# A Winograd residual block: first loads in one order with three in flight, half of image 2's squares on ScalarE, embedding weights in the staging buffers, and a new instruction order

## The chip, the cores and the metric

One Trainium2 chip, one core of it. The metric is the device time of one execution in microseconds. Before the change it is 475.57 us, the median of 3 runs (474.12 to 476.09).

## The reference

A residual block of a diffusion network on x of 2 images x 512 channels x 64 x 64, in bfloat16. `gn` is a group norm over 4 groups of 128 channels, `conv3` a 3x3 convolution from 512 to 512 channels with zero padding.

```python
h = conv3(silu(gn(x, g1, be1)), w1)
emb = silu(t_emb) @ w_emb              # t_emb: 2 x 1152, w_emb: 1152 x 512
h = h + emb.reshape(B, C, 1, 1)
h = conv3(silu(gn(h, g2, be2)), w2)
return x + h
```

A group of the norm is one channel tile of 128 channels, the partitions of the chip. So the mean and the mean square of a channel tile are sums along its 4096 pixels and over its partitions.

## The kernel before

**Tiling.** There are 4 channel tiles (ct) on the input side and 4 (ot) on the output side. An image is cut into 2 chunks of 32 rows, so each convolution ("layer") has 4 chunks, and each chunk 4 groups, one for each ot: 32 groups in all. The convolution is done by a Winograd scheme along the rows (4 output rows from 6 transformed rows, "pos" 0 to 5), and for some positions also along the columns ("nested"). The transformed activations of a chunk are V, made by VectorE and ScalarE; the transformed weights are U, made from the raw weights R and a third tap g1t. Positions 0 and 5 use R itself.

**The work of a chunk's V** (`produce_V`): for each channel tile, a load into `ak` (chunk 0 uses the x that is there already, `xbuf`), the SiLU with the norm's scale and bias on ScalarE (L571), a scaling by -4 (L578 and L584 through the helper at L300/L301), an addition (L585), a subtraction (L592), a doubling, then the rows of V (L612, L622) and its column differences (L632, L637). There are two V buffers: a chunk's V begins when the last matmul of the chunk two before has read its own. `xbuf` takes the first of them at the start.

**The work of a weight block's U** (`prep_U`, one for each pair of channel tiles): loads of g1t (L393) and R (L394), scalings (L300/L301), an addition that is a DMA of GpSimd (L424) or VectorE's, and two additions on VectorE (L413). g1t stays in one of 3 staging buffers ("stage") until its last addition.

**Scaled copies.** The string FLIP says for each scaled copy, in the order in which the program is written, whether ScalarE (L300) or VectorE (L301) does it.

**The norm's statistics.** For image 1 (`stats0`) and image 2 (`gn1_stats`) TensorE computes the Gram matrix of a channel tile's pixels in 32 matmuls of 128 columns (L354); VectorE takes its diagonal (L363), the sum of squares. 32 matmuls against a column of ones give the sums (L359). For channel tile 0 of image 1 ScalarE makes the sums (L703). `gn_scale_bias` turns both into scale and bias: a matmul over the partitions (L311), a few small steps of VectorE (L313 to L328) and a power on GpSimd (L326). Image 2's pixels come in 8 pieces of 512 KB into the 5 slots of `ring` (`gn1_load`, L477). They wait for the last load of image 1, and a slot's second piece for those who read the first.

**The output of a group.** ScalarE or VectorE moves the sums out of PSUM (`rm`), VectorE combines rows into `ring` slots 0 to 2 (y) and 3 and 4 (z), GpSimd adds z to y with a DMA (L983), and SP stores y to `h_scr` (L987). In layer 0 ScalarE then sums y and its squares (L748).

**The embedding.** w_emb comes in 5 loads (four of 256 KB, one of 128 KB, L451) into stretches of a V buffer that its chunk does not use, one before each of the groups 2 to 6. `emb_mm` multiplies them one group later (L460).

**The order.** Each engine executes its instructions in a fixed order. A table ORDER, one list of ranks for each of TensorE, VectorE, ScalarE, GpSimd and SP, was written down beforehand and is laid over the program by `in_order`. SP issues nearly all loads and stores, so a wait in front of one holds up all that stand behind it. There are 8 semaphores for SP's and ScalarE's DMAs, and a DMA that takes a semaphore again waits for the landing of the one before.

SP's first loads stand in this order: the two halves of image 1's channel tile 0 (512 KB each), tiles 1 and 2 (1 MB each), R of the first weight pair, tile 3, g1t of the first pair, R and g1t of the second.

Of the kernel before, what the change touches and what calls it, by code (L numbers as in the profile page):

```python
# [10 lines left out]
ALU = mybir.AluOpType  # L11
# [7 lines left out]
class _Background:  # L19
# [45 lines left out]
0-31 34 66 35-38 32 39-46 33 47-60 67-95 61-65 96-97 99-106 98 107-158 164-167 159-162 168-194 163 195 228 196-227  # L65
230-242 294 229 300-302 243 295-299 303-304 382 306-308 305 385 309 383 386 310 384 311 244-291 376 292-293 377 387
378 388 379-381 458-461 389 462-463 390 312-354 467 355-364 464 391-393 365-375 470-475 540 465 541 466 552-553 542
394-414 554 415 555 543-545 416-456 556-557 457 468-469 546-548 476-539 549-551 558 582 559 583 560 584 561-565
585-592 566-570 593 606-611 618-619 612-617 620 571-574 594 575-577 595-596 578-581 597-605 621 630 622-625 631
646-648 626 662-667 627-629 668-675 649-654 676-677 655-661 632-635 678-680 636-640 681-684 641-642 685 687-690  # L70
643-645 691 699-704 692 705 693-696 706 686 711-713 727 707-708 743 709-710 697 744 714 745 715-721 698 722-726
746-754 728-742 755-756 775-776 787 777 757-763 767 788-790 768 764-766 791-795 778 796-797 799 779 800 798 801-806
815 780-783 807 784 808-810 816-817 785 769 811-812 770 818 786 819-820 813-814 821-823 771-773 824 774 825-858
863-868 859 869-874 887 903 888 904-908 889-892 909-912 893 860-862 913 875-881 919 882 920 883 921 914-917 922-923
918 924-926 894 884-886 927-928 895-899 929 900-902 930-932 951-955 933-936 963 937-942 964-966 956 967 957 968 958
969 943-944 970 975-976 959 991 960 971 961-962 992 945 972 946-950 993-996 973 997-998 974 999 977 1000 1007-1017
1039 1051 1018-1021 1001 1022-1029 1002 1030 1003-1004 1040-1043 978 1005-1006 1044 979-981 1045 982 1052 1046 983
1053 984-990 1047 1054 1048-1049 1055-1056 1050 1057-1060 1031-1038 1061 1063-1067 1079 1068 1095 1062 1096-1111
1069 1112 1070-1078 1113-1118 1080-1094 1123 1135-1138 1119 1139 1120-1122 1140-1142 1124-1128 1147 1129 1148-1153
1163-1171 1154-1156 1172-1174 1157-1162 1130 1175 1143 1131 1176-1178 1144-1145 1132-1133 1146 1134 1179-1181  # L80
1195-1203 1182-1184 1204-1210 1185-1194 1211 1223-1225 1212-1218 1226-1231 1219-1222 1232-1239 1251 1240-1250
1252-1272 1283-1298 1273-1279 1299-1301 1311 1280-1282 1302-1305 1312-1313 1306-1307 1314-1316 1308 1317 1323 1339
1355 1340-1354 1318-1319 1309-1310 1320-1322 1324-1338 1356-1365 1387 1366-1368 1388 1369 1371-1381 1370 1382-1384
1399 1385-1386 1389 1400 1411-1413 1401 1414-1416 1402 1427 1443 1428-1430 1417 1431-1436 1418-1426 1437-1442 1444
1403 1445-1452 1404-1405 1390-1392 1406-1410 1393-1398 1459-1466 1475 1467-1474 1453-1458 1476-1477 1488-1496
1500-1501 1497-1498 1502 1499 1516-1524 1503-1515 1478-1487 1525-1526 1532 1527-1531 1533-1536 1564-1569 1576
1537-1541 1577-1580 1548-1563 1542-1547 1581 1570 1582 1571-1573 1583-1587 1574-1575 1588-1590 1604 1591-1594
1605-1608 1595-1603 1609-1635 1652-1655 1664 1656 1665 1657 1636-1651 1666-1669 1658-1660 1676-1677 1670 1678
1671-1672 1679 1673-1674 1680-1686 1692-1694 1687-1688 1695-1696 1708-1709 1689 1697-1704 1690 1710 1705-1706 1691
1707 1675 1661-1663 1711-1739 1764-1765 1740-1750 1766 1751-1757 1767-1768 1758-1759 1769 1760 1770 1761-1763  # L90
1771-1780 1796-1799 1781 1800-1801 1782 1802-1804 1783-1795 1828 1805-1806 1829 1812 1830-1831 1813 1807-1809 1832
1810 1814-1823 1811 1824-1827 1852 1833-1834 1840 1853-1854 1835-1836 1841-1842 1837-1838 1843-1845 1868 1846 1839
1869-1871 1847-1850 1872-1873 1855-1856 1851 1874-1877 1857-1862 1884 1863-1867 1885-1907 1878-1883 1932-1934
1908-1912 1935-1944 1920-1921 1945-1947 1922-1928 1913 1929-1931 1948-1953 1964-1966 1954-1957 1914-1919 1967
1958-1963 1968-1985 1988-1992 1986-1987 1993-1997 2000 1998 2001-2005 2012-2013 2028 2014-2016 2044-2046 2017
2029-2032 2006 2033-2035 2018-2022 1999 2036 2023-2024 2037-2038 2025 2039-2041 2047 2042 2007-2011 2026-2027
2048-2056 2068-2070 2080 2071-2073 2043 2074 2057 2075-2077 2081-2083 2078-2079 2058-2067 2084-2086 2092-2093
2108-2110 2087 2094 2088-2090 2124-2125 2091 2126-2131 2111-2114 2095-2098 2132 2099 2115 2133 2100-2102 2116-2120
2103 2121-2123 2134 2104 2149 2105-2107 2150-2153 2161-2162 2135 2163 2154 2164 2148 2165 2173-2174 2136-2140 2175
2141-2144 2166 2145-2147 2167-2168 2155-2156 2169-2170 2189 2171 2157-2160 2176 2190-2191 2177-2180 2192 2181-2186  # L100
2193 2187 2205 2194 2188 2195 2172 2206-2210 2196-2204 2211 2221-2236 2212-2220 2237-2240 2249-2250 2241-2242
2251-2252 2243-2244 2253-2254 2245 2255 2246-2248 2256-2261 2277 2262-2267 2293 2268-2270 2278-2281 2271-2275 2325
2276 2282-2292 2294-2305 2337 2306 2326 2338-2339 2307-2308 2340 2327-2331 2341 2309-2324 2349-2361 2365-2370
2362-2363 2371-2375 2342 2364 2376 2381-2382 2377-2380 2343 2332-2336 2344 2383-2385 2345-2348 2386-2412 2437
2413-2427 2438-2443 2428-2430 2453-2460 2469 2461-2468 2444-2452 2431-2436 2470-2478 2501-2503 2479-2484 2504-2508
2485-2500 2509-2510 2513-2515 2511 2525-2526 2516-2518 2512 2519-2520 2527 2521-2522 2541-2542 2557-2559 2528 2543
2529-2532 2523 2533 2560 2544 2561-2562 2545 2524 2546-2547 2534-2536 2548-2549 2537-2538 2550 2539 2551-2552 2540
2553-2556 2563-2572 2589-2595 2573-2576 2601-2605 2577-2588 2596-2598 2613-2615 2599-2600 2606-2610 2629-2630
2645-2646 2631 2647-2648 2611 2649 2612 2616-2628 2650-2660 2632-2644 2677-2679 2689 2661-2673 2690-2691 2674-2676
2692-2694 2680 2695-2698 2681 2701-2705 2699 2682-2683 2700 2684-2688 2706 2717-2719 2733-2737 2720-2722 2738-2739  # L110
2723-2726 2707-2708 2740-2742 2709-2716 2727-2732 2743-2753 2765-2767 2754-2755 2768-2773 2756-2764 2774 2789-2790
2777 2775-2776 2791-2797 2778-2779 2805-2806 2798-2799 2780 2800 2807-2810 2801 2781 2802-2803 2782-2783 2821-2825
2784-2786 2826 2804 2787-2788 2827-2833 2811-2820 2853-2856 2837 2857-2859 2838-2839 2865 2840-2841 2877-2879
2834-2835 2866-2868 2860-2863 2836 2842-2847 2880-2885 2848-2852 2886 2864 2887-2892 2869-2875 2893 2909 2894
2910-2916 2895-2896 2917 2897-2906 2918-2919 2907-2908 2920-2922 2876 2923-2940 2965-2966 2941-2945 2953-2964 2981
2997 2967 2982 2998-3000 2946-2952 3001 2968-2969 3002 2970-2978 3029-3035 2983-2986 2979-2980 2987-2989 3036-3037
2990 3038-3040 2991-2996 3041-3042 3003-3007 3013 3008-3009 3053-3058 3014 3059-3063 3010-3012 3015-3028 3064-3068
3043-3044 3069 3045-3049 3070 3085-3086 3071-3072 3087 3073 3050-3052 3074-3075 3088-3097 3076-3084 3101-3107
3181-3182 3108-3116 3183-3184 3098-3100 3193-3194 3185-3188 3195 3117-3126 3133 3149 3127-3128 3134-3135 3129-3131
3136 3150 3137 3151 3138-3139 3132 3140-3148 3189 3152-3155 3165-3168 3156 3169-3180 3157-3164 3205-3206 3190-3192  # L120
3196-3198 3207-3208 3229 3209 3199-3202 3230-3231 3210 3203-3204 3211 3232 3212-3216 3233-3234 3217-3228 3235-3252""",
    "DVE": """
0 4 3 1-2 6 50 5 7-13 15 14 27 26 17 47 28 48 29 49 30 51 16 20 33-34 31 52 32 35 53 36 18 37 41 40 19 38 54 22 39
42 55 43 56 44 57 21 45 78 46 23 58 24 59-60 25 61-62 101-102 63 70 64 71 81 65 85 66 103 98 106 67-68 104 69 108
105 79 82 72-73 80 107 127 111 109 83 110 84 112 167 86 74-75 124 87-89 76-77 90 125 92 126 93 91 129 94 130 95 128
96 132 97 134 131 136 135 133 99 137 100 113 138 114 140 117 115 139 141 121-123 145-146 116 147 118-120 148 161 143
# [59 lines left out]
def kernel(  # L186
# [491 lines left out]
    for ct in range(CT):  # L678
# [7 lines left out]
        if ct < 2:  # L686
            next(gens_U0[ct])
# [451 lines left out]
```

## Time and profile before

| | |
|---|---|
| median of 3 runs | 475.57 us |
| the profiled execution, its own time | 475.3 us |
| its span from the first to the last instruction | 473.3 us |
| TensorE (PE) busy | 452.2 us, 96% |
| VectorE (DVE) busy | 424.6 us, 90% |
| ScalarE (ACT) busy | 364.5 us, 77% |
| mean granted TensorE clock | 0.996 |
| gram matmuls of image 2 (L354, aux<-ring) | 128, 9.6 us busy |
| squares and sums of y on ScalarE (L748) | 32, 61.2 us busy, 1913 ns each |

A line of the timeline has the start, the duration, the engine, the source line, the operation, out<-in, the shapes and the count of what was merged; in brackets the idle time of the engine before it and what ended that. A matmul's duration (0.38 us for 512 columns) is its latency; the next one starts earlier, so the rate is read from many in a row. Lines of the windows have the busy time of PE, PEld (weight loads), DVE, ACT and POOL with the number of instructions, then the granted clock, the DMA share and GB/s.

### The profile page before, as it was taken

The page shows a single profiled execution, that of the slowest core. Times are in us where ns is not written, and L with a number is a line of the kernel's source. Part 1 is how long each engine was busy: PE and PEld are TensorE (multiplying, and loading weights), DVE is VectorE, ACT ScalarE, POOL GpSimd, SP SyncE. Part 2 cuts the span into 40 slices and gives each one's busy share as a digit, 9 for nine tenths or more (in the row PEclk, how much of TensorE's full clock was granted, in tenths as well). Part 3 has the DMA queues.
Part 4 walks back from the last instruction along what each step waited for, and adds up shares of the span by engine and source line. Part 5 has one row for each costly group of instructions (what it writes and reads, how often), then busy time and mean ns, then how long its engine had stood idle before and what let it go on. Part 6 is the DMA issues. An engine that isn't in the chain of part 4 may idle for free. (4 is left out here: it accounts for less than half of the span.)

```text
span 473.3 us, 8439 instructions
## 1 busy us (share of the span) xinstructions
PE 452.2 (96%) x3260; PEld 291.7 (62%) x3260; DVE 424.6 (90%) x811; ACT 364.5 (77%) x394; POOL 76.7 (16%) x119
## 2 busy tenths in 40 slices
PE   4987999999999999999989999989999999999996
PEld 3945645555555666667656555446766676675774
DVE  0899999989989899989999999998999999975576
ACT  4489959998979789789999999737878666644462
POOL 1122210300000000020221122113211221212010
PEclk9998999999999999999999999999999999999999
DMA  8898785555462181638679896567856778549372
GB/s 305 289 355 246 173 169 145 159 158 145 136 180 46 56 216 48 178 91 238 154 163 260 210 225 139 128 134 169 215 125 167 180 168 192 133 98 191 112 176 91
DMA packets 30833, 80.03 MB, mean 169 GB/s; under 512 B 2763, under 2 KB 15691, under 8 KB 30411
## 3 DMA queue, kind: packets, MB, share of 16 engines
q0 software_dynamic: 11872, 34.87, 36.5%
q1 hardware_dynamic: 18864, 44.64, 28.2%
q8 instruction: 25, 0.41, 0.3%
q14 instruction: 13, 0.11, 0.1%
q10 hardware_dynamic: 59, 0.01, 0.0%
HBM read 42.54 MB, written 16.78 MB: 125 GB/s over the span
## 5 line engine op out<-in xcount | busy, mean ns | idle before, releaser
L886 PE MATMUL nst<-V,U 128*128 128x256 f16 x1600 | 203.8, 271 | 4.5 <-ACT rm L300 2.6
L878 PE MATMUL acc<-V,R 128*128 128x512 f16 x744 | 193.3, 384 | 2.8 <-DVE V L612 1.9
L886 PEld LDWEIGHTS <-U 128*128 128x128 f16 x1600 | 153.7, 96 | 51.3 <-issue 2.8
L878 PEld LDWEIGHTS <-R 128*128 128x128 bf16 x792 | 76.2, 97 | 72.2 <-issue 4.0
L300 ACT ACTIVATE rm<-nst 128x1024 f16<-128x1024 f32 x97 | 96.5, 1022 | 27.6 <-PE nst L886 18.6
L878 PE MATMUL mid<-V,U 128*128 128x512 f16 x336 | 86.1, 385 | 3.2 <-DVE V L622 2.9
L748 ACT ACTIVATE ring<-ring 128x2048 f16<-128x2048 f16 x32 | 61.2, 1913 | 4.2 <-issue 2.1
L571 ACT ACTIVATE ak<-ak,nb_all,sc_all 128x2112 f16<-128x2112 f16 (+1 forms) x28 | 60.2, 2149 | 0.8 <-DMA ak<-h_scr 0.8
L878 PEld LDWEIGHTS <-U 128*128 128x128 f16 x336 | 32.3, 97 | 41.6 <-issue 6.6
L300 ACT ACTIVATE ring<-ring 128x512 f16<-128x512 f16 x46 | 27.3, 625 | 25.1 <-DVE ring L945 13.0
L300 ACT ACTIVATE ak<-ak 128x520 f16<-128x520 f16 (+1 forms) x34 | 35.5, 1060 | 11.2 <-DVE ak L592 8.2
L983 POOL DMA_DIRECT2D ring<-ring x28 | 26.0, 928 | 110.6 <-ACT ring L300 90.5
L585 DVE TENSOR_TENSOR ak<-ak 128x2080 f16<-128x2080 f16 x32 | 39.5, 1234 | 1.2 <-issue 0.9
L622 DVE TENSOR_TENSOR V<-ak 128x1040 f16<-128x1040 f16 x54 | 38.2, 708 | 0.3 <-ACT ak L300 0.2
L933 DVE TENSOR_TENSOR rm<-tu,rm 128x1024 f16<-128x1024 f16 x50 | 34.2, 683 | 3.7 <-ACT rm L300 3.5
L300 ACT ACTIVATE U<-R 128x768 f16<-128x768 bf16 (+1 forms) x29 | 31.8, 1128 | 1.5 <-DMA R<-in_w_dram 1.5
L300 ACT ACTIVATE ring<-acc 128x512 f16<-128x512 f32 x52 | 29.5, 594 | 1.7 <-DVE ring L952 1.1
L637 DVE TENSOR_TENSOR V<-V 128x1024 f16<-128x1024 f16 (+1 forms) x54 | 30.7, 577 | 0.0
L413 DVE TENSOR_TENSOR U<-U,g1t 128x1536 f16<-128x1536 f16 x32 | 30.2, 945 | 0.4 <-DMA U<-U 0.4
L932 DVE TENSOR_TENSOR tu<-rm 128x512 f16<-128x512 f16 x50 | 20.8, 417 | 10.1 <-ACT rm L300 10.0
L632 DVE TENSOR_TENSOR V<-V 128x2048 f16<-128x2048 f16 (+1 forms) x27 | 27.5, 1019 | 0.0
L931 DVE TENSOR_TENSOR tu<-rm 128x512 f16<-128x512 f16 x50 | 20.8, 417 | 6.4 <-ACT rm L300 6.4
(120 smaller groups left out, 417.8 us busy)
## 6 DMA issues: line engine op xcount, KB each, us to landing
ring<-ring POOLq DMA_DIRECT2D x28, 512.0 KB, 4.7
ak<-h_scr SPq DMA_DIRECT2D x16, 528.0 KB, 4.7
h_scr<-ring SPq DMA_DIRECT2D x16, 512.0 KB, 4.0
ring<-in_x_dram POOLq DMA_DIRECT2D x14, 512.0 KB, 5.5
out_dram<-ring POOLq DMA_DIRECT2D x14, 512.0 KB, 5.1
ak<-in_x_dram SPq DMA_DIRECT2D x12, 528.0 KB, 4.5
R<-in_w_dram SPq DMA_DIRECT2D x16, 384.0 KB, 7.0
U<-U POOLq DMA_DIRECT2D x14, 384.0 KB, 5.4
```

Of the source, the lines that this page charges most:

```text
L300: return nc.scalar.activation(out=o, in_=i, func=ACT.Copy, scale=f)
L413: nc.vector.tensor_tensor(out=o, in0=i0, in1=i1, op=op)
L571: nc.scalar.activation(out=at[:, lo - r0:hi - r0, 1:W + 1], in_=sap, func=ACT.Silu, bias=nb_all[:, layer, b, ct:ct + 1], scale=sc_all[:, l ...
L585: nc.vector.tensor_tensor(out=diff, in0=diff, in1=below, op=ALU.add)
L622: nc.vector.tensor_tensor(out=o, in0=in0, in1=in1, op=op)
L632: nc.vector.tensor_tensor(out=lo2.rearrange("p c q (t w) -> p (q t) c w", w=HALF), in0=plane_pair(0, HALF + 2), in1=plane_pair(1, HALF), o ...
L637: nc.vector.tensor_tensor(out=hi2[:, c].rearrange("p q (t w) -> p (q t) w", w=HALF), in0=i0, in1=i1, op=op)
L748: behind(nc.scalar.activation(out=junk, in_=y, func=func, scale=scale, accum_out=acc), inst)
L878: nc.tensor.matmul(out, lhsT=w_direct(pos, ct, kx), rhs=rhs, start=first, stop=last)
L886: nc.tensor.matmul(accs["nst", (pos - 1) // 2][bank][:, q, :, plane, :], lhsT=lhsT, rhs=rhs.rearrange("p (t w) -> p t w", w=HALF), start=s ...
L933: nc.vector.tensor_tensor(out=msl[:, 1 - k:4 - k:2].rearrange("p q t w -> p q (t w)"), in0=tu[:].rearrange("p q t e w -> p q (t e w)"), in ...
L983: add_z = lambda: nc.gpsimd.dma_start(out=flat(yst), in_=ring[:, NY + turn % NZ], accum_op=ALU.add)
```

## The change

1. **First loads.** All loads of image 1 and of the first two weight pairs go through `load`, which keeps them in one order and lets each wait for the landing of the third before it. Channel tiles 1 to 3 come in halves too. The order is: tile 0 (two halves), R and g1t of the first pair, tile 1, R and g1t of the second pair, tile 2, tile 3.
2. **Squares.** For channel tiles 1 and 3 of image 2 ScalarE squares the two pieces in place and sums them (4 passes over 128 x 2048). Their 64 gram matmuls and two of the diagonal steps go; VectorE adds the two partial sums. The sums by TensorE stay.
3. **Embedding weights.** Nine loads of 128 KB, each into a staging buffer of its own, instead of five in V. Staging buffers go round among g1t and these.
4. **Order and factors.** ORDER and FLIP are new. VectorE has 795 instructions instead of 803, ScalarE 371 instead of 359. In TensorE's list one sum over image 2's first piece stands ahead of the first convolution matmul, where 13 gram matmuls stood, and the transpose of the norm's parameters stands ahead of the second channel tile's statistics.

```diff
-    def prep_U(layer, ot, pr, eng=None, dep=None):
+    def prep_U(layer, ot, pr, load=None, dep=None):
...
-        q = eng or nc.sync
-        after(q.dma_start(out=g1t[:], in_=w[:, :, 6 * P:9 * P]), dep() if dep else None)
-        after(q.dma_start(out=R[:].rearrange("p c a b o -> p c (a b o)"), in_=w[:, :, 0:6 * P]),
-              dep() if dep else None)
+        ld = load or (lambda o, i: after(nc.sync.dma_start(out=o, in_=i), dep() if dep else None))
+        ld(R[:].rearrange("p c a b o -> p c (a b o)"), w[:, :, 0:6 * P])
+        ld(g1t[:], w[:, :, 6 * P:9 * P])
...
     def emb_load(i):
         n = min(EMB_PIECE, ET - i * EMB_PIECE)
-        o = i % (CT - 1) * VCT + VFLAT
-        wt = Vt[(0, 0, 1)][:, o:o + EMB_PIECE * C].bitcast(BF16).rearrange("p (e o) -> p e o", o=C)
-        nc.sync.dma_start(out=wt[:, 0:n, :], in_=wemb_v[:, i * EMB_PIECE:i * EMB_PIECE + n, :])
+        wt = []
+        for j in range(n):
+            t = stage.tile([P, 2 * NKX * P], BF16, tag="stage", name="wt")
+            nc.sync.dma_start(out=t[:, 0:C], in_=wemb_v[:, i * EMB_PIECE + j])
+            wt.append(t)
...
-        gram_pe(pcs, b0[:, 0:P])
         sums_pe(pcs, b1)
-        me_gram(me[:, 1, ct:ct + 1], b0[:, 0:P])
+        if SQ_ON_ACT(ct):                       # ct % 2 == 1
+            parts = sq_all[:, 2 * ct:2 * ct + 2]
+            for k, pc in enumerate(pcs):
+                nc.scalar.activation(out=pc, in_=pc, func=ACT.Square, scale=float(HW) ** -0.5,
+                                     accum_out=parts[:, k:k + 1])
+            nc.vector.tensor_tensor(out=me[:, 1, ct:ct + 1], in0=parts[:, 0:1], in1=parts[:, 1:2], op=ALU.add)
+        else:
+            gram_pe(pcs, b0[:, 0:P])
+            me_gram(me[:, 1, ct:ct + 1], b0[:, 0:P])
...
+    def load(o, i):
+        inst = nc.sync.dma_start(out=o, in_=i)
+        if loads:
+            behind(inst, loads[-1])
+        if len(loads) >= IN_FLIGHT:             # 3
+            after(inst, loads[-IN_FLIGHT])
+        loads.append(inst)
+        return inst
+
+    gens_U0 = [prep_U(0, 0, pr, load=load) for pr in range(NPAIR)]
     for ct in range(CT):
         xt = xbuf[:, ct * HW:(ct + 1) * HW]
-        np_ = 2 if ct == 0 else 1
-        pcs = [xt[:, k * HW // np_:(k + 1) * HW // np_] for k in range(np_)]
+        pcs = [xt[:, k * HW // 2:(k + 1) * HW // 2] for k in range(2)]
         for k, pc in enumerate(pcs):
-            x_dma[(0, ct)] = nc.sync.dma_start(out=pc, in_=x_v[0, ct][:, k * HW // np_:(k + 1) * HW // np_])
+            x_dma[(0, ct)] = load(pc, x_v[0, ct][:, k * HW // 2:(k + 1) * HW // 2])
...
-        if ct < 2:
-            next(gens_U0[ct])
+        for pr in W0_AFTER.get(ct, ()):         # {0: (0,), 1: (1,)}
+            next(gens_U0[pr])
```

## The prediction

> **What bounds the kernel now.** I read the page first (busy shares, the span in 40 slices), then the timeline of the first 70 us, the windows, and the waits of TensorE.
>
> ```profile
> PE 452.2 (96%) x3260; PEld 291.7 (62%) x3260; DVE 424.6 (90%) x811; ACT 364.5 (77%) x394; POOL 76.7 (16%) x119
> ...
> PE   4987999999999999999989999989999999999996
> ...
> DVE  0899999989989899989999999998999999975576
> ACT  4489959998979789789999999737878666644462
> ```
>
> TensorE is the bound, with VectorE close behind; both are nearly full from slice 5 on. TensorE's loss is at the start, so that is where the change has to be priced. The timeline shows it:
>
> ```profile
> 4.87 1.89 PE L354 MATMUL gm<-xbuf 128*128 128x128 bf16 x16 [4.87 <-DMA xbuf<-in_x_dram]
> ...
> 20.05 1.67 PE L354 MATMUL ga<-xbuf 128*128 128x128 bf16 x27
> ...
> 23.76 0.39 PE L878 MATMUL mid<-V,U 128*128 128x512 f16 x1
> ...
> 28.69 0.38 PE L878 MATMUL acc<-V,R 128*128 128x512 f16 x1 [1.85 <-DVE V L612]
> ...
> 37.97 0.60 PE L878 MATMUL mid<-V,U 128*128 128x512 f16 x2 [2.88 <-DVE V L622]
> ...
> 40.61 3.10 PE L354 MATMUL aux<-ring 128*128 128x128 bf16 x32
> ...
> 53.59 1.95 PE L354 MATMUL aux<-ring 128*128 128x128 bf16 x32
> ...
> 56.84 5.70 PE L878 MATMUL mid<-V,U 128*128 128x512 f16 x25
> ```
>
> The first convolution matmul starts at 23.76. Then TensorE waits twice for V, which VectorE makes, and pays once more for the second wait: 32 gram matmuls take 3.10 us at 40.61 and 1.95 at 53.59. The windows show the rest:
>
> ```profile
> 30.00:35.00 5.00, 5.00 (x65) 3.16 (x64) 4.81 (x7) 5.00 (x5) 1.52 (x2) 1.00 1.10 332
> 35.00:40.00 5.00, 1.89 (x8) 0.72 (x7) 4.92 (x11) 5.00 (x5) 0.28 (x1) 0.96 1.03 320
> 40.00:45.00 5.00, 5.00 (x60) 4.04 (x59) 5.00 (x11) 5.00 (x7) 1.14 (x2) 0.70 0.81 194
> 45.00:50.00 5.00, 5.00 (x50) 3.02 (x49) 5.00 (x14) 5.00 (x6) 1.21 (x1) 1.00 0.92 262
> ```
>
> Columns: PE, PEld, DVE, ACT, POOL busy, granted clock, DMA share, GB/s. From 30 to 50 VectorE and ScalarE are full, TensorE has 3.1 us idle, and the clock falls to 0.70 after that.
>
> **An account of TensorE.** Matmuls follow each other every 0.222 us at 512 columns (25 in 5.70, the last one's own 0.39 off), 0.110 at 256, 0.061 for a gram (32 in 1.95) and 0.029 for a column of sums. Behind 23.76 the program has 1600 at 256 columns (175.4), 1080 at 512 (239.5), 48 halves (5.4), 115 grams (7.0), 128 sums (3.8) and small ones (3.3): 434.4 us. The last matmul ends at 469.3, 445.5 later, so 11.1 us are idle or slow: 2.0 at 26 to 28, 3.4 at 35 to 38, about 1 in slow clock, and 5 in pieces up to 2.2 us between 225 and 365. A tail of 4.0 to the span's 473.3 and 2.0 outside it make the profiled 475.3, 0.3 under the median of 475.57.
>
> **Squares on ScalarE.** They remove 64 gram matmuls from TensorE: 64 x 0.061 = 3.9 us, and TensorE has no idle time from 41 to 225 for that to fall into. They add four passes on ScalarE over 128x2048, each like the L748 squares (1.91 us): 7.6 us in a stretch in which ScalarE is full. VectorE loses two L363 (0.36 each) and gains two small sums (0.16 each). The new factors move eight scaled copies net from VectorE to ScalarE over the whole run (0.3 to 0.7 us each there, 0.6 to 1.8 here); I price that at 0, since ScalarE is 23% idle and most of it falls behind 60 us; if that cover failed it would be a few tenths each. What is queued behind the squares on ScalarE: the first two stand behind the scaling for channel tiles 2 and 3 of chunk 0, the last two ahead of the first activation of chunk 1, now at 47.95. The reload of the last ring piece waits for the second square instead of TensorE.
>
> **First loads.** Now R of the first weights is issued at 4.84 and lands at about 14.2 (9.4 us is the median of its kind), so VectorE begins to scale U at 14.20, although it idled 8.8 us before 9.87. In the changed order this weight load is third, beside only two halves of x, and lands at about 6.5 (the first 1.4 MB have moved by then: 174 GB/s to 5.0, 404 after). So scaling U (0.36, 0.56, 0.35) and the first U additions (three of 0.95) fall into time in which VectorE now waits. The second half of channel tile 0 shares with less and lands near 6.3 instead of 7.8; its ScalarE sum then ends at 8.9 (it follows the first's 1.91) instead of 9.8. The gparm transpose also stands ahead of the second gram set, so its 1.25 us wait is gone. The scale of channel tile 0 comes at 8.9 + 0.2 (adding the halves) + 0.9 (over TensorE, as now) + 1.8 (two U additions inside the chain) + 1.5 (its small steps, as now) = 13.3 instead of 14.06, with three U additions done. At the first scaling of the activated tile by -4 (now 16.56) I put the new kernel at 16.1 with 1.6 us more VectorE work behind it: VectorE stands 2 to 3 us better. The work ahead of chunk 0's last V pair is 31 us in both orders; it ends at 44.7 now, so at 41.5 to 42.
>
> The price: each later load waits for the third before it. 5.4 MB at 400 GB/s would be through at 16, as now (the wait for x ends at 16.49); four rounds of the least landing time that the trace has for x (4.1 us, plus 0.44 to issue) give 18.9. I take 18, nearer to the second, since the traffic falls when few loads are in flight:
>
> ```profile
> 16.00:18.00 2.00, 2.00 (x20) 2.00 (x19) 2.00 (x4) 0.46 (x1) 0.16 (x1) 1.00 0.38 129
> ...
> DMA to landing us min/median/max: 4.1/6.6/8.7
> ```
>
> (129 GB/s just after x has landed, then the landing times of x.) The loads of image 2 start behind that, and the new order puts one sum over their first piece ahead of the first convolution matmul; it lands at 18 + 4.1 to 5. The statistics of x take TensorE from the landing of channel tile 1 (about 10.2; now 10.39) for 12.4 us as now. Both give 22.5 to 23: **first convolution matmul at 22.8**, instead of 23.76.
>
> The Trainium skill speaks against this part (DMA: Bandwidth & Descriptors, section Bandwidth: batch to 1 MiB or more, its table has 341 GB/s at 1 MB and 138 at 64 KB), since halves replace whole tiles and few are in flight. Estimated with 250 to 340 GB/s from that table, x would be through at 18 to 23.5 and the sum would come out at 469 to 474. Here half-megabyte pieces ran at 404 GB/s between 5 and 10 us, with more in flight.
>
> **Embedding weights.** Nine loads of 128 KB in the staging buffers instead of five in V. Each waits for the staging tile three before it, and on SP's queue chunk 1's loads of channel tiles 2 and 3 and the stores of h stand behind the first two. Those waits are for U additions of ot 2 and 3, which VectorE has done about 61 to 72 us in; the loads behind need 5 to 6 us and are activated now at 73.8 and 78.3. I price it at 0, between -0.5 (V is free of them) and +3 (one load's worth of lateness in chunk 1).
>
> **Sum.** From the first convolution matmul the new order has 175.4 + 239.5 + 5.4 + 64 grams (3.9) + 127 sums (3.7) + 3.3 = 431.2. Idle time up to chunk 1: counted along the built orders with these durations, the first matmuls of channel tiles 1, 2 and 3 stand behind 6.5, 12.4 and 16.2 us of TensorE work, so at 29.3, 35.2 and 39.0; VectorE has their first V at 28, 34 and 38.5. Nearly no wait there. Chunk 1's last V op stands behind 83.0 us of VectorE work (82.1 now, ended at 98.2, so 16.1 idle before it). With 10.5 idle at the start and 2.5 to 4.5 later it ends at 96 to 98; TensorE could use it at 92.5. I book 3.5 us idle there instead of the present 6, and 5.2 later as now: behind chunk 1 the new order has the same groups, and each V still starts when TensorE frees its buffer. 22.8 + 431.2 + 3.5 + 5.2 + 4.0 + 2.0 = 468.7; with the 0.3, **469.0**, 1.4% faster. Ends: first matmul at 22.0, 0.5 and 4 idle: 464. First matmul at 24.5, 6.5 and 7 idle: 475.5.
>
> **Rivals.** (1) *The start loses nothing*: V and U come so early that TensorE runs through. For it: the work per V above fits within 1 us. Against: VectorE gets no slack to absorb a late transfer. 468.7 - 3.5 - 0.5: 465. (2) *ScalarE becomes the bound of chunk 1*: it is full to 60 us, and 7.6 us of squares less 3 us of earlier start put chunk 1's activations 4.6 later. Then chunk 1's V ends at 98 to 100 as now, and only TensorE's smaller rest counts (361.3 us behind that point instead of 363.1): 473.5 to 475. Against: half of the squares stand where ScalarE idled or had U work that could wait. (3) *Slower, by the first loads*: the waits cost full round trips. If each of four rounds takes the median landing of 6.6 us plus 0.5, x is through at 29; statistics and image 2's first piece end near 33, and TensorE starts 9 us late with 3.2 less to do and its waits as now: 481. It decides from a last landing of x at about 25 on. Against: 404 GB/s while the first three pieces are in flight.
>
> **Chances.** Within 0.5% (2.4 us) is about what a measurement of this kernel cannot tell from no change. Forecast 0.62 (465.5 to 472.5); rival 1 0.10, faster too; rival 2 0.18 (0.07 faster, 0.09 same, 0.02 slower); rival 3 0.10 (0.07 slower, 0.03 same where it is mild). Faster 0.79, same 0.12, slower 0.09. The range 464 to 475.5 takes in the ends of the unknown costs and most of rival 2, and leaves out rival 3 and a little at either side.
>
> **What would show it.** Right: first L906 matmul near 22.8; no wait of 2 us before 45 and no clock under 0.9 there; the 72nd convolution matmul (end of the first group) near 47 instead of 57; chunk 1 begun before 97. Wrong: x through after 22 us, a wait of ScalarE's activations for chunk 1 on its loads, or idle TensorE of over 6 us before 100.

## The result, and the profile after

The changed kernel takes 478.01 us in the median of 14 runs (476.13 to 479.25); the kernel before, run beside it, takes 475.83 us. The ratio is 1.0046, with a 95% interval of 1.0024 to 1.0068. So the change made the kernel slower, by an amount just inside the 0.5% that the text above called no change. The forecast was 469.0, 1.4% faster. The profiled execution has 478.48 us and a span of 476.5.

The page, as far as it answers to the lines shown of before (PEclk is TensorE's granted clock in tenths):

```profile
PE 451.8 (95%) x3196; PEld 289.1 (61%) x3196; DVE 421.1 (88%) x801; ACT 381.5 (80%) x410; POOL 75.6 (16%) x119
...
PE   3799998999999999999899998999999999999996
...
DVE  3587998999999999989899999998999799965576
ACT  5478998999889999879899989747787798944562
...
PEclk9559999999999999999999999999999999999999
```

TensorE has 64 matmuls less, and ScalarE 17 us more work (7.6 of it the squares, the rest scaled copies). In the first two slices VectorE works where it idled before (0 8 became 3 5), and TensorE's clock is at half in slices 2 and 3. TensorE's timeline (start, duration, engine, line, operation; in brackets the idle time before) shows the start:

```profile
4.90 3.44 PE L364 MATMUL gm<-xbuf 128*128 128x128 bf16 x32 [4.90 <-DMA xbuf<-in_x_dram]
...
11.85 0.29 PE L364 MATMUL ga<-xbuf 128*128 128x128 bf16 x1 [2.30 <-DMA xbuf<-in_x_dram]
...
18.55 1.03 PE L364 MATMUL gm<-xbuf 128*128 128x128 bf16 x8 [2.28 <-DMA xbuf<-in_x_dram]
...
22.01 0.40 PE L364 MATMUL ga<-xbuf 128*128 128x128 bf16 x2 [0.54 <-DMA xbuf<-in_x_dram]
...
28.94 0.59 PE L906 MATMUL mid<-V,U 128*128 128x512 f16 x1
```

It waits for x at tiles 1, 2 and 3, and the first convolution matmul starts at 28.94, not at 22.8 as forecast nor at 23.76 as before. SP's queue shows why; of the kernel before:

```profile
0.74 1.93 SPq L683 DMA_DIRECT2D xbuf<-in_x_dram  x4
...
16.49 1.46 SPq L477 DMA_DIRECT2D ring<-in_x_dram  x2
```

and of the changed kernel:

```profile
13.51 5.34 SPq L698 DMA_DIRECT2D xbuf<-in_x_dram  x4
23.22 0.80 SPq L488 DMA_DIRECT2D ring<-in_x_dram  x2
```

The loads of image 2 (ring) wait for the last piece of x, so their issue tells when x is through: 16.49 before, 23.22 now. Before, four loads with 3 MB together were under way by 2.7 us. Now the last four halves of x go out between 13.5 and 18.9, each when the third load before it has landed. The windows give the rate (last column, GB/s; the granted clock is two columns ahead of it). Of the kernel before:

```profile
5.00:10.00 5.00, 3.65 (x32) 3.11 (x30) 0.14 (x2) 3.85 (x4) 0.00 (x0) 1.00 1.03 404
10.00:15.00 5.00, 4.61 (x64) 4.39 (x65) 2.06 (x13) 0.69 (x1) 0.56 (x1) 1.00 1.01 399
```

and of the changed kernel:

```profile
5.00:10.00 5.00, 3.84 (x35) 3.45 (x35) 2.38 (x10) 4.62 (x5) 0.00 (x0) 1.00 0.76 252
10.00:15.00 5.00, 3.15 (x42) 3.16 (x43) 2.46 (x7) 0.46 (x1) 0.56 (x1) 0.64 0.70 238
15.00:20.00 5.00, 2.72 (x38) 2.64 (x36) 2.73 (x7) 4.53 (x4) 0.16 (x1) 0.50 0.85 276
...
30.00:35.00 5.00, 5.00 (x14) 1.69 (x13) 5.00 (x16) 4.39 (x4) 1.10 (x2) 0.50 1.03 389
35.00:36.00 1.00, 1.00 (x12) 0.49 (x11) 1.00 (x3) 0.29 (x2) 0.00 (x0) 0.84 1.05 368
```

252 and 238 GB/s, where the kernel before had 404 and 399.

**Where the time went.** With the cadences of the prediction, each trace splits into the time up to the first convolution matmul, the work from there to chunk 1's first matmul (the first nested one of that chunk, `nst`), the idle or slow time in that stretch, and the same behind it (us, one execution each):

| kernel | first matmul | idle to chunk 1 | chunk 1 begins | idle behind | own time |
|---|---|---|---|---|---|
| before | 23.8 | 5.2 | 99.2 | 6.0 | 475.3 |
| changed | 28.9 | 4.2 | 102.2 | 7.7 | 478.5 |
| forecast | 22.8 | 3.5 | | 5.2 | 468.7 |

Against the kernel before: 5.2 later at the start, 3.1 less work, 0.7 more idle, 0.5 more tail (4.5): 3.3 slower by these rounded figures. Against the forecast: 6.1 at the start, 3.2 idle or slow (11.9 instead of 8.7), 0.5 in the tail: 9.8.

### The profile page after: what moved, and what is told of

The parts are those of the page before. It is cut to its first block, busy times and chain, and to the rows that moved or that the text cites. A ratio compares the mean times of both kernels' runs of the same rounds, so it can differ in the third digit from the quotient of the medians.

```text
span 476.5 us, 8316 instructions
## 1 busy us (share of the span) xinstructions
PE 451.8 (95%) x3196; PEld 289.1 (61%) x3196; DVE 421.1 (88%) x801; ACT 381.5 (80%) x410; POOL 75.6 (16%) x119
## 4 chain that ended last, share of the span: by engine, by line
PE 62%; ACT 11%; DMA 11%; DVE 9%; issue 5%; POOL 0%; DVEq 0%; SPq 0%; ACTq 0%; POOLq 0%
PE acc L906 24%; PE nst L914 23%; PE mid L906 11%; DMA ring<-ring 4%; DMA xbuf<-in_x_dram 4%; ACT rm L310 3%; ACT ring L310 2%; ACT ring L776 2%; ACT ak L310 1%; DMA ak<-h_scr 1%; ACT ak L589 1%; DVE ak L603 1%; PE half L906 1%; DVE V L640 1%; DMA R<-in_w_dram 1%
## 5 line engine op out<-in xcount | busy, mean ns | idle before, releaser
L914 PE MATMUL nst<-V,U 128*128 128x256 f16 x1600 | 209.4, 271 | 3.5 <-ACT rm L310 2.4
L906 PE MATMUL acc<-V,R 128*128 128x512 f16 x744 | 195.7, 385 | 3.9 <-ACT ring L310 3.0
L906 PE MATMUL mid<-V,U 128*128 128x512 f16 x336 | 90.6, 390 | 0.6 <-DVE U L422 0.6
L310 ACT ACTIVATE ak<-ak 128x520 f16<-128x520 f16 (+1 forms) x40 | 46.0, 1157 | 6.8 <-DVE ak L610 4.7
L310 ACT ACTIVATE ring<-ring 128x512 f16<-128x512 f16 x52 | 30.9, 622 | 19.8 <-DVE ring L975 10.9
L960 DVE TENSOR_TENSOR tu<-rm 128x512 f16<-128x512 f16 x50 | 20.8, 417 | 11.7 <-ACT rm L310 11.6
L433 POOL DMA_DIRECT2D U<-U x14 | 17.2, 1227 | 66.4 <-DVE V L655 11.3
```

Source lines behind the costliest of these rows:

```text
L310: return nc.scalar.activation(out=o, in_=i, func=ACT.Copy, scale=f)
L906: nc.tensor.matmul(out, lhsT=w_direct(pos, ct, kx), rhs=rhs, start=first, stop=last)
L914: nc.tensor.matmul(accs["nst", (pos - 1) // 2][bank][:, q, :, plane, :], lhsT=lhsT, rhs=rhs.rearrange("p (t w) -> p t w", w=HALF), start=s ...
```

## The experiments

Each variant was timed beside the kernel before; the ratio to it, with its interval, is what is compared. Theory A: the limit on the first loads made the start late, and that is the loss. Its rivals: ScalarE's squares and the embedding loads hold chunk 1 back, so that an earlier start gains nothing (B); the half clock that follows from the waits is the loss (C), against which D says that a faster TensorE would only wait for x and V.

**1. More loads in flight.**

```diff
-    IN_FLIGHT = 3
+    IN_FLIGHT = 4        # flight4; 6 in flight6; 14 in flight14
```

> The changed kernel with four of the first loads in flight instead of three; nothing else differs. Theory A (the limit of three costs the start: x is through at 23.2 us and the first convolution matmul comes at 28.9 instead of 23.8, and TensorE's clock, which needs unbroken work to rise, is granted in full only at 35.3): x through at 19 to 20.5, first convolution matmul at 25 to 26, full clock earlier than 32, time 474 to 476. Rival B (chunk 1 is held back by ScalarE's squares and by the embedding loads on SP's queue, so an earlier start only turns into longer waits there): the start moves as in A, TensorE's idle time between 55 and 103 us grows by what the start gains, time 477.5 to 479.

> The changed kernel with six in flight. Theory A: DMA near 400 GB/s as in the kernel before, x through at 16.5 to 17.5, first convolution matmul at 22.5 to 24, time 470 to 473; R of the first pair lands one to three us later than with three (7.6). Rival B: 477 to 479, idle time of TensorE between 55 and 103 of 6 us or more instead of 2.8.

> The changed kernel with no limit of its own on the first loads (one order, and only the eight semaphores of SP's and ScalarE's DMAs). Theory A: x through at 16 to 17, time within 1.5 us of six in flight. If the order of arrival is what the limit was good for (all pieces share the bandwidth and the first tile lands late), the scale of channel tile 0 comes later than 14.5 and the time is 1 to 3 us above six in flight.

| in flight | GB/s at 5 to 10, 10 to 15 | x through | first matmul | chunk 1 | median | ratio to before |
|---|---|---|---|---|---|---|
| 3 (the change) | 252, 238 | 23.2 | 28.9 | 102.2 | 478.01 | 1.0046 (1.0024 to 1.0068) |
| 4 | 327, 304 | 21.2 | 26.9 | 101.7 | 474.14 | 0.9983 (0.9957 to 1.0009) |
| 6 | 381, 386 | 18.6 | 24.5 | 96.7 | 472.61 | 0.9951 (0.9931 to 0.9972) |
| 14 | 367, 362 | 18.9 | 23.5 | 98.5 | 473.10 | 0.9958 (0.9937 to 0.9979) |

The rates, the last load and the first convolution matmul with six:

```profile
5.00:10.00 5.00, 4.06 (x43) 3.69 (x42) 2.60 (x11) 4.42 (x5) 0.00 (x0) 1.00 1.02 381
10.00:15.00 5.00, 2.75 (x66) 2.67 (x64) 2.85 (x10) 2.79 (x2) 0.57 (x1) 1.00 1.05 386
...
18.64 0.80 SPq L488 DMA_DIRECT2D ring<-in_x_dram  x2
...
24.48 0.59 PE L906 MATMUL mid<-V,U 128*128 128x512 f16 x1
```

Theory A holds. One number takes the kernel from 0.46% slower to 0.49% faster: 0.95%, 4.5 us. Rival B falls, since the earlier start is not given back (from 55 to 103 us TensorE waits 1.5 us with six, where B wanted 6 or more; it is 2.3 with three). R of the first pair lands at 7.21 with six and at 7.34 without a limit (7.60 with three), so the limit did not speed it up either. Nor was the order of arrival what it was good for: without a limit the scale of channel tile 0 is ready at 13.0, not after 14.5, and the time is within 0.5 us of six. The expected places were missed: x came 0.7 us (four), 1.1 us (six) and 1.9 us (no limit) later than the latest that was expected, the first matmul 0.9 and 0.5 us (four and six), and R with six not later but earlier. The times of all three lay in their ranges. The traced executions with four, six and no limit took 477.29, 474.55 and 474.65 us, each more than the median beside it, so their places of chunk 1 are late for these medians: the row of four has chunk 1 only 0.5 us earlier than the change, though its median is 3.9 us lower. With six the bulk of x is there by 16.5 and the last piece trickles in until 18.6, at 74 GB/s and less; so the first matmul stays 0.7 us behind the kernel before.

**2. The number of loads, or their bytes?** The kernel before with a limit of three on its nine loads, tiles 1 to 3 of x being loads of 1 MB (before_three), and with these tiles in halves too (before_halves3, twelve loads); the changed kernel with tiles 1 to 3 whole (after_tiles).

```diff
 # before_three: nine loads, line = SP's own order of them
+    for k in range(3, 9):
+        after(line[k], line[k - 3])
 # before_halves3: the same over twelve loads, and
-        np_ = 2 if ct == 0 else 1
+        np_ = 2
 # after_tiles, for ct > 0
-            x_dma[(0, ct)] = load(pc, x_v[0, ct][:, k * HW // 2:(k + 1) * HW // 2])
+            x_dma[(0, ct)] = load(xt, x_v[0, ct])
```

> The kernel before with one thing added: each of its nine first loads waits for the landing of the third before it (whole tiles of 1 MB as before, in its own order). Theory A, by the number of loads in flight: x through at 20 to 23 instead of 16.5, time 478 to 482. Theory A, by the bytes in flight (three of 1 MB are twice as much as three halves): x through at 17 to 19, time 475.5 to 478. Rival B: x later by any of these, time within 1 us of the kernel before, since its chunk 1 has slack for it.

> The kernel before with image 1's channel tiles 1 to 3 in halves and each of its twelve first loads waiting for the third before it; order of the loads, squares, embedding and plan are its own. If at most 1.5 MB in flight is what the changed kernel lost by: first load of image 2 issued at 21 to 24 us instead of 16.5, first convolution matmul at 27 to 29, time 477.5 to 480. If the kernel before has slack in its chunk 0 (its TensorE waits 5.4 us for V there): the same late start, but 474.5 to 476.5.

> The changed kernel, still three in flight, but channel tiles 1 to 3 of image 1 come as one load of 1 MB each instead of two halves. If the bytes in flight decide (three loads then hold up to 3 MB instead of at most 1.5): about 390 GB/s from 5 us on, the first load of image 2 issued at 17 to 19 instead of 23.2, first convolution matmul at 23.5 to 25.5, time 472.5 to 474.5. If the number of loads or the waits themselves decide: first load of image 2 after 21, time 476 to 479.

before_three: 406 and 391 GB/s, x through by 16.1, 475.67 us, ratio 1.0021 (1.0000 to 1.0043). before_halves3: 348 and 303 GB/s, x through by 19.0, 479.93 us, ratio 1.0101 (1.0075 to 1.0127). after_tiles: 282 and 288 GB/s, x through at 20.8, 473.81 us, ratio 0.9988 (0.9965 to 1.0012).

Three loads in flight cost 0.2% (hardly told from nothing) where they hold up to 2.5 MB (two tiles and half of another), and 1% where they hold at most 1.5 MB, in a kernel that has none of the other parts of the change. So the bytes in flight count, not the number of loads; nor is it the size of one load, since six of the same halves ran at 381 GB/s. after_tiles lies in the time that this gave, though its rate was not the 390 GB/s that I expected, and x came at 20.8 instead of 17 to 19: a limit that counts loads also gives slots to g1t, of 192 KB, and from 8.4 to 12.3 us at most one tile, one R and one g1t were in flight, 1.6 MB. before_halves3 had x earlier than the expected 21 to 24, and its first matmul is only 1.4 us later than in the kernel before (25.2, expected 27 to 29), but chunk 1 begins at 103.5 instead of 99.2. So the time is as the theory has it and its path only in part. The loss grows by 2.9 us behind the first matmul. The first wait for V there is as before, but the second is 3.75 us instead of 2.88, a wait of 0.8 us for VectorE's reading of the statistics is new, and the clock is at half from 39.3 to 46.1, where the kernel before has that from 39.6 to 43.0:

```profile
29.84 0.38 PE L897 MATMUL acc<-V,R 128*128 128x512 f16 x1 [1.84 <-DVE V L622]
...
40.31 3.57 PE L897 MATMUL mid<-V,U 128*128 128x512 f16 x8 [3.75 <-DVE V L632]
...
40.00:45.00 5.00, 4.69 (x21) 2.41 (x21) 5.00 (x13) 5.00 (x6) 1.42 (x2) 0.50 0.98 317
```

**3. The half clock.** In the changed kernel the clock is at half from 11.4 to 35.3 us (windows above; from 30 to 35 TensorE does 14 matmuls in 5 us). Additional matmuls fill TensorE's waits for x.

```diff
+    FILL = ((44, 33), (56, 97), (24, 119))     # after_fill; ((10, 33), (40, 97), (20, 119)) in flight6_fill
+        for n, anchor in FILL:                 # n of them behind TensorE's instruction "anchor"
+            for _ in range(n):
+                nc.tensor.matmul(bank[:, 256:384], lhsT=ident[:], rhs=ident[:], start=True, stop=True)
```

> The changed kernel with 124 matmuls of 128 columns added to TensorE's list where it waits for x (44 ahead of channel tile 1's Gram matrix, 56 ahead of tile 2's, 24 ahead of tile 3's); their results are not read. They change nothing but TensorE's idle time, so they ask what the half clock from 11.4 to 35.3 us costs. Theory C (it costs what it slows: statistics of tiles 2 and 3, and 6.4 us of convolution at half rate): full clock from about 8 to 40, first convolution matmul at 26 to 27.5, time 474 to 475.5. Rival D (the start is paced by the landing of x and by V; a faster TensorE only waits for V): first convolution matmul no more than 2 us earlier, new waits for V of 2 us or more before 60, time 477 to 478.5.

> Six in flight and 70 such matmuls (10, 40 and 20), whose results are not read. With six the clock is granted in full from about 10 to 15.4 and then half until 29.1. Theory C: full from 10 on, first convolution matmul at 22 to 23, time 469.5 to 471. Rival D: waits for V before 45 come instead, time 472 to 473.

The windows of after_fill have the full clock:

```profile
20.00:25.00 5.00, 5.00 (x109) 5.00 (x107) 3.85 (x14) 0.25 (x1) 1.40 (x1) 1.00 0.44 139
...
30.00:35.00 5.00, 5.00 (x74) 3.63 (x73) 5.00 (x12) 4.22 (x4) 0.94 (x1) 1.00 1.01 374
```

From 30 to 35 TensorE does 74 matmuls instead of 14. The first convolution matmul comes 1.9 us earlier (27.1; 0.5 of it because x was through at 22.7 in that execution), and the time stays: 477.78, ratio 1.0062 (1.0033 to 1.0092) against 1.0046. flight6_fill: 472.05, ratio 0.9942 (0.9915 to 0.9969) against 0.9951. Theory C falls: the half clock costs nothing that these runs can tell (by the two intervals at most about 1 us with three in flight, where C wanted 2.5 to 4; with six they leave room for 2). Rival D has the time right and the place only in part. Of the 1.9 us, 1.9 are still there at chunk 1 (100.3), and the idle time behind it grows by 1.5 (9.2 instead of 7.7) in the one execution that was traced.

**4. Squares back on TensorE,** with six in flight.

```diff
-    SQ_ON_ACT = lambda ct: ct % 2 == 1
+    SQ_ON_ACT = lambda ct: False       # 64 grams placed behind the sums of their tile
```

> Six in flight, and the squares of channel tiles 1 and 3 of image 2 go back to TensorE: 64 gram matmuls behind the sums of their tile, no squares on ScalarE, VectorE reads the two diagonals where it added the partial sums. If the squares were worth what the forecast said (64 x 0.061 us of a TensorE that has no idle time there): 475.5 to 476.5, 3.2 to 3.9 above six in flight. If ScalarE's 7.6 us cost as much as TensorE saves (rival 2 of the forecast): 472 to 473.5, and ScalarE has idle time between 45 and 65 that it does not have with the squares.

The first form came out at 481.28, ratio 1.0148 (1.0113 to 1.0184), by a wait of its own:

```profile
45.08 0.16 PE L386 MATMUL aux<-ones_bf,ring 128*128 128x1 bf16 x1 [7.43 <-DVE aux L390]
```

VectorE read the diagonals late and so held the bank of PSUM that these matmuls write. Mended:

> Squares of channel tiles 1 and 3 back on TensorE with six in flight, as in flight6_grams, but VectorE reads the two diagonals soon after their matmuls instead of where it added ScalarE's partial sums, so that the bank is free in time. (flight6_grams came out at 481.3, but TensorE stood 7.4 us at 37.6 us in for a bank that VectorE's late reading held; that wait is this edit's own and belongs to neither theory.) If the squares are worth the forecast's 3.9 us of TensorE: 475.5 to 476.5. If ScalarE's 7.6 us cost as much (rival 2): 472 to 473.5. If more than TensorE's time hangs on them: above 477.

475.72 us, ratio 1.0001 (0.9975 to 1.0027). Against six in flight (0.9951) the squares on ScalarE are worth 0.5%, 2.4 us (3.1 by the medians; the intervals leave 0.8 to 4.0); the forecast had 3.2 of work saved. In the windows from 45 to 65 ScalarE is busy 10.67 of 20 us without the squares and 19.77 with them. It had the room, and rival 2 falls. TensorE's wait for a bank is not all gone in the mended form (1.6 us ahead of 42.5), so 2.4 is, if anything, too much.

**5. ScalarE's order behind chunk 1.** TensorE waits there for copies that ScalarE makes late. Of six in flight, the waits of TensorE from 100 us on (us in total, times, longest):

```profile
PE acc L906 <- ACT ring L310: 4.5, 3, 1.7
PE nst L914 <- ACT rm L310: 2.6, 1, 2.6
```

```diff
 # ORDER["Activation"], with IN_FLIGHT = 6
-... 174-175 173 176 ...   230 206 203 209 ...   211-213 232 219 214 ...   274 283 280 282 ...   48 47 46 55 53
+... 174 173 175-176 ...   230 203 206 209 ...   211-213 219 232 214 ...   274 280 283 282 ...   48 47 55 46 53
```

> Six in flight and five places of ScalarE's list changed, nothing else: copies out of PSUM (rm<-nst, ring<-acc) stand ahead of an instruction that waits for a DMA or for VectorE, at about 74, 230, 267, 283 and 349 us of six in flight, where TensorE waits for exactly these copies (1.3, 2.6, 1.3, 1.5 and 1.7 us). If ScalarE's order is what TensorE loses there: 2 to 4 us less of such waits, time 468.5 to 471. If VectorE, full from 240 to 320, is behind it: the waits come later under V or U, time 471.5 to 473.

```profile
PE acc L906 <- ACT ring L310: 2.6, 3, 1.1
PE acc L906 <- DVE ring L311: 2.4, 1, 2.4
```

The copy that TensorE waited 2.6 us for (at 233.3) now comes in time, and TensorE waits 2.4 us for one of VectorE's a little further on (at 237.1). 473.99 us, ratio 0.9979 (0.9966 to 0.9993): not faster than six in flight, and later than either theory said.

**6. Image 2 earlier as well,** on top of experiment 5.

```diff
-            after(nc.sync.dma_start(out=xt, in_=...), x_dma[(0, CT - 1)])
+            after(nc.sync.dma_start(out=xt, in_=...), x_dma[(0, CT - 2)])
-    last_x0 = lambda: x_dma[(0, CT - 1)]
+    last_x0 = lambda: x_dma[(0, CT - 2)]
```

> flight6_act with the loads of image 2 and of the next weights waiting for channel tile 2 of image 1 instead of tile 3 (six in flight: last piece of tile 3 seen at 18.6, DMA nearly idle from 16.5 on). First load of image 2 issued at 16 instead of 18.6. If the start still counts: 0.5 to 2 us below flight6_act. If TensorE is paced by the statistics of x: the same within 0.7.

The first load of image 2 goes out at 16.2, and the first matmul starts at 24.9 as without it. 472.44 us, ratio 0.9952 (0.9929 to 0.9974): 1.5 us below flight6_act, and the same as six in flight alone. That is the time expected if the start still counts, but the start did not move and the intervals of the two overlap, so no cause is shown for it. Six in flight (or no limit, which the runs cannot tell from it) is the simplest version that beats both kernels.

## Why the prediction was wrong

**The step that failed: x through at 18.** The price of the limit was put at four rounds of the least landing time of the trace (4.1 us). The chain of the changed kernel is R of the first pair, landed at 7.60; the second half of tile 1, landed at about 13.5; the first of tile 2, at about 18.5; the last of tile 3, at 23.2. So the rounds begin at 7.6 and take 4.7 to 5.9 us each; in the forecast the four together end at 18.9, of which it took 18. The 4.1 us belong to the very first load, and I set this price against a false reading: "404 GB/s while the first three pieces are in flight". In the kernel before four loads with 3 MB were in flight by 2.7 us (the first SP line above), twice the bytes that three halves hold. The estimate from the Trainium skill (DMA: Bandwidth & Descriptors, section Bandwidth) had x through at 18 to 23.5; the trace agrees, with 23.2, at its late end. It agrees in the number only: the table goes by the size of a load (of loads that GpSimd issues, where SP does here), and the same halves ran at 381 GB/s with six in flight. Of the forecast's own signs of being wrong, the first, x through after 22, is what came.

**First matmul at 22.8** failed with it: 28.9. It was the sum's largest miss, 6.1 of 9.8 us: 5.2 by the late x, and the rest because the statistics behind it ran at half clock (5.7 us from there to the first matmul, 4.4 in after_fill).

**Rival 3 is what happened,** in a milder form than its 6.6 us rounds (x at 29, TensorE at 33, 481). The point from which it was said to decide, a last landing at about 25, was too late: 23.2 was enough. Its chance of 0.10 rested on the same false reading.

**R and U earlier.** R landed at 7.60 (forecast 6.5), the second half of tile 0 at 6.59 (6.3), and the scale of tile 0 was ready at 13.2 (13.3). That holds, but the -4 scaling came at 17.46 instead of 16.1. ScalarE's new list puts a scaling of the second pair's R ahead of the first activation, and that R landed at 14.5:

```profile
14.54 0.84 ACT L310 ACTIVATE U<-R 128x768 f16<-128x768 bf16 x1 [4.89 <-DMA R<-in_w_dram]
15.29 2.13 ACT L589 ACTIVATE ak<-xbuf,nb_all,sc_all 128x2112 f16<-128x2112 bf16 x1
```

I had followed VectorE's and TensorE's lists past the late load, not ScalarE's.

**Squares** were right in size and cover (2.4 to 3.1 us measured, 3.2 forecast), as far as the noise lets one say.

**Embedding weights** at 0: no run takes this part out alone. In the traces of the changed kernel and of six in flight no activation waits for a load of chunk 1, which speaks for 0.

**Idle to chunk 1:** with the limit lifted it is 3.1 us with six (5.8 with fourteen), where 3.5 was booked and the kernel before has 5.2. With three it is 4.2, so some of the step came, but one execution of each, from 3.1 to 5.8 with the same lists, does not show how much.

**Idle behind chunk 1, "5.2 as now":** too small. By the table's count the nine traced kernels with the new lists unchanged on ScalarE behind chunk 1 have 6.6 to 9.7, 7.7 in the mean; the three with the old lists have 5.4 to 6.3. That is about 1.8 us, from one execution each; the 9.7 is from an execution that took 1.9 us more than its kernel's median. (The forecast had drawn the line a little elsewhere, 6 and 5.2 for the kernel before; the sum is the same.) The same work in another order has other waits, and I had carried the old ones over. The five places of ScalarE's list that flight6_act moved are not what makes them; what does is left open.

**The sum, by runs.** The limit costs 0.95% (4.5 us), the squares bring 0.50% (2.4 us), and all the rest, order, early R, embedding weights and factors, brings nothing (1.0001 with both taken out). The forecast had 3.4 us for that rest: 6.6 in all, less the 3.2 of work. So the miss of 9.0 us is the limit (4.5), this rest (3.4, in which the forecast had its own price of the limit taken off) and what the squares fell short (0.8), to within 0.3. The rest was to be an earlier first matmul (1.0) and less idle time up to chunk 1 (2.5). The first did not come even with six in flight (24.5 against 23.8), and by the traces the second is offset by the idle time behind.

## What to carry to other kernels

A limit on loads in flight has to be priced by the bytes that it leaves in flight, and the rate to price it with is that of a stretch with as many bytes under way, not the best rate of the trace. Follow a late load through every engine's list: one instruction that needs it holds up all that stand behind it, whatever they need. And a planned order is new in all its waits: the idle time of the old plan is a poor estimate for it, even far behind the change.

## What was not expected of the hardware

The rate of large loads moved with the bytes in flight over a wide range: 252 GB/s (5 to 10 us) with three loads of at most 512 KB, 327 with four, 381 with six, 406 with three of up to 1 MB each (at most 2.5 MB).

TensorE's clock stayed at half long after the waits: in the changed kernel TensorE works without a pause that the profile shows from 22.0, and the full clock is granted at 35.3, 13.3 us later. The Trainium skill (TensorE: Matmul & The Clock Gate, section on the HAM clock gate) has the full clock after some 3.4 us of sustained work; this trace differs, and the measurement decides. Other traces lie on both sides: from the last pause before it, the full clock took 12.0 us with four in flight, 3.6 without a limit and 1.3 in after_tiles. What decides it no run here shows. At the start of a trace the clock column reads 1.00, though 32 grams took 3.44 us at 4.90 (0.107 each, as at half clock) and 1.95 where the clock is full: there the matmuls' own cadence is what to read.
